# Late x transposes by DMA, K chunks of 128 rows, and score fills shared by two head groups, in a gated attention and MLP kernel on one core

## The chip, the cores and the metric

The kernel runs on one core of one Trainium2 chip. The metric is the device time of one launch in microseconds (us), lower is better. Engines are called PE (TensorE), PEld (its weight loads), DVE (VectorE), ACT (ScalarE), POOL (GpSimd) and SP (SyncE, whose queue issues most DMAs).

## The reference, cut to what matters

```python
# x: 2048 tokens of 448 numbers, bfloat16; 16 heads of 28; four segments of 512 tokens
g = sigmoid((x * gate_w).sum(-1))
a = memory_attention(x, wq, wk, wv, wo, beta)
b = token_mlp(x, w1, b1, w2, b2)
return g * a + (1 - g) * b

# memory_attention, per segment s and head:
logits = q @ k.T / sqrt(28) + causal mask; p = softmax(logits); a_dot = p @ v
a_mem  = phi(q) @ M / (phi(q) @ z)            # phi(t) = t + 1 if t > 0 else exp(t)
o      = sigmoid(beta) * a_mem + (1 - sigmoid(beta)) * a_dot
M += phi(k).T @ v;  z += phi(k).sum()          # carried to the next segment
# then o @ wo

# token_mlp: over the token axis, S = 2048 -> F = 1792 -> S
h = layernorm(x);  u = gelu(h.T @ w1 + b1);  y = u @ w2 + b2
```

The input of the MLP is x itself, so the MLP's first matmul needs only the layernorm of x and the first block of W1. It is the large independent pool of PE work (224 matmuls of the first, 224 to 238 of the second layer) that the kernel places between the pieces of attention.

## The kernel before

The program is written as a list of operations with priorities. A list scheduler in the kernel's own source, with assumed durations, fixes the order on every engine when the program is built. Each engine is given its order as a fixed list: if one operation is late, what stands behind it on that engine is late too (the ACT lines at 28 us, further down, show a wait of 0.74 us passed on in this way).

x is loaded in natural layout (128 tokens on the partitions). Its transpose, needed by the Q, K and V projections, is made on PE against an identity, in four groups of 512 tokens, and copied out of PSUM, the memory that PE writes to, by DVE or ACT. The 448 rows of the contraction are cut in four chunks of CK = 112.

```python
def transposes(tc):                                   # tc = 0..3
    for half in range(2):
        ...
        for ti, c in parts:                           # 8 matmuls
            last = e.matmul(tb[0:CK, at : at + 128], xh[:, 4 * tc + ti, c * CK : c * CK + CK], ident[:, :],
                            is_transpose=True, ...)
        ...                                           # copy of 112 x 1024 by DVE or ACT
```

The layernorm works in place on the same tiles xh, hence after the transposes. One step on POOL computes the coefficients for all sixteen tiles.

```python
def ln_stats(t):  DVE: bn_stats(st6[:, t, :], xh[:, t, :]); bn_aggr(mv[:, t, :], st6[:, t, :])
def ln_coef():    POOL: vpe = var + 1e-5; rstd = vpe ** -0.5; nmr = -mean * rstd      # 128 x 16, all tiles
def ln_apply(t):  DVE: xh[:, t, :] = xh[:, t, :] * rstd[:, t] + nmr[:, t]
```

Attention runs in 16 units, u = (segment, group of 4 heads). Four heads share PE as row tiles of 32 rows, each writing its own PSUM bank of 512 columns. A unit has 1280 causal columns per head and needs three fills of the four banks: 512, 384 + 128, and only 256 in the last. ACT takes the exponential of each fill into an SBUF buffer P (two halves, by parity of u), POOL masks the diagonal blocks, and PE, as column tiles of 32, multiplies P with v.

```python
def scores(n):
    u, f = divmod(n, 3)                               # three fills per unit
    ...
    PE : for j, c0, w_ in segs(f): for hl in range(4): matmul(bank(hl)[:, c0 : c0 + w_], kT[...], qT[...])
    ACT: activation(pv, ps[:, 0:4, 0:w], Exp, scale=SCALE)          # 128 x 2048 or 128 x 1024
    POOL: affine_select(...)                                        # the diagonal blocks
def pv_unit(u): ...                                   # P @ v, the memory term, normalisation, transpose
```

## Time and profile before

| | before |
|---|---|
| time, median of 3 runs (range) | 189.0 us (188.65 to 189.43) |
| profiled execution, span | 186.4 us |
| PE, DVE, ACT busy | 97%, 83%, 72% |
| exponentials, number and busy time | 48, 76.9 us |
| PE transposes of x | 64 |
| first projection, first MLP matmul start | 7.80 us, 34.29 us |

The first part of the page gives busy time, share of the span and number of instructions of each engine.

```profile
PE 180.6 (97%) x1373; PEld 87.3 (47%) x1384; DVE 154.0 (83%) x319; ACT 133.5 (72%) x171; POOL 69.6 (37%) x93
```

The chain that ended last, before: the share of the span that each engine, and each line, has on it.

```profile
PE 82%; DVE 6%; ACT 6%; DMA 3%; issue 1%; SPq 0%
PE t L889 24%; PE t L917 24%; PE t L589 9%; PE t L783 7%; PE t L869 6%; PE t L820 6%; PE t L646 3%; ACT t L792 3%; DMA t<-in_A_wk_dram 3%; DVE t L732 2%; PE t L670 1%; ACT t L631 1%; PE t L558 1%; DVE t L581 1%; DVE t L624 1%
```

So PE sets the time. But "97% busy" is not "97% streaming". The Trainium skill, "Trainium Kernel Development and Optimization", Performance Expectations, calls matmul busy time a bad metric because matmuls are pipelined, and this trace agrees: a matmul of 448 columns is shown with 353 ns, while the next starts 189 ns later. The useful account is made from the starts. I took every matmul of the trace as its columns at 2.4 per ns (56 ns for a 128-column transpose or a 128-column matmul of the full array, as their starts stand) and called the rest up to the next start a gap. The record of before lacks 11 of its 12 matmuls of the memory term (their weight loads are there, see the groups below); they are put back at 512 columns.

The groups of instructions by line and shape, before. The columns are number, busy us, mean ns, idle time of the engine before them, with what ended it. L792 is the exponential, L558 the PE transpose, L581 and L583 the copies of the late transposes, L806 the memory term.

```profile
L792 ACT ACTIVATE t<-t 128x2048 bf16<-128x2048 f32 x32 | 60.3, 1886 | 9.5 <-PE t L783 9.2
...
L792 ACT ACTIVATE t<-t 128x1024 bf16<-128x1024 f32 x16 | 16.5, 1032 | 3.0 <-PE t L783 3.0
...
L558 PE MATMUL t<-t 128*112 128x128 bf16 x64 | 4.5, 220 | 0.1
...
L583 ACT ACTIVATE t<-t 112x1024 bf16<-112x1024 bf16 x3 | 3.1, 1024 | 0.5 <-PE t L558 0.5
L581 DVE COPY t<-t 112x1024 bf16<-112x1024 bf16 x3 | 2.1, 692 | 0.1
L806 PEld LDWEIGHTS t<-t 128*128 128x128 bf16 x12 | 1.2, 97 | 1.9 <-DVE t L688 0.4 <-issue 0.3 <-POOL t L796 0.2
...
L806 PE MATMUL t<-t 128*128 128x512 bf16 x1 | 0.4, 379 | 0.0
```

The timeline of PE around one score fill, before (start, duration, engine, line, shape, number). The fill streams 384 + 128 columns on four row tiles at once.

```profile
42.64 0.73 PE L889 MATMUL t<-t 128*128 128x448 bf16 x3
43.30 0.40 PE L783 MATMUL t<-t 28*128 28x384 bf16 x8
43.63 0.74 PE L889 MATMUL t<-t 128*128 128x448 bf16 x3
```

The last MLP matmul of the first row starts at 43.02 us and streams to 43.20; the fill starts at 43.30, has streamed 512 columns by 43.53, and the MLP goes on at 43.63. About 0.10 us is lost on the way into the tiled mode and again on the way out. The Trainium skill, "TensorEngine Tiling (Array Packing)", Key Properties, says that a change of the tiling mode drains TensorE; the trace agrees and gives the size.

The start of the chain in order of time, before: wk lands at 6.13 us, DVE copies it into its padded form (L536), then come two copies of the first transposes and the first projection (L589).

```profile
1.31 4.82 DMA t<-in_A_wk_dram
...
6.16 0.63 DVE t L536
6.79 0.34 DVE t L571
...
7.15 0.61 ACT t L574
...
7.80 4.31 PE t L589 x33
```

### The profile page before, as it was taken

To read this page: it belongs to the slowest core of one execution; us is meant where nothing else is said; L and a number is where in the kernel's file an instruction comes from. 1 tells how busy PE (TensorE), PEld (TensorE's weight loads), DVE (VectorE), ACT (ScalarE), POOL (GpSimd) and SP (SyncE) were. 2 spreads that over 40 slices of the span, in tenths; PEclk is the share of its full clock that TensorE was granted. 3 is DMA by queue.
4 is the path that set the end of the run, shared out by engine and by line. 5 is a ranking of instruction groups with operands and counts; after the bars stand their busy time and mean duration, and the time that the engine had idled before them with its cause. 6 is when DMAs were issued, how large, how long until landed. Compare 5 with 4: busy or idle time off the path is not lost.

```text
span 186.4 us, 3493 instructions
## 1 busy us (share of the span) xinstructions
PE 180.6 (97%) x1373; PEld 87.3 (47%) x1384; DVE 154.0 (83%) x319; ACT 133.5 (72%) x171; POOL 69.6 (37%) x93
## 2 busy tenths in 40 slices
PE   7999999999999999999999999999999999999994
PEld 2658434344454444434454443454454444454554
DVE  1979898998689989798998999998999987765232
ACT  2288779968999999999988979840399857620230
POOL 8200029343242534543725635171135365160200
PEclk9999999999999999999999999999999999999999
DMA  3999991001971746001341506238810072744011
GB/s 92 321 328 265 294 150 28 5 0 40 250 220 31 204 116 159 4 4 28 96 133 37 160 4 183 45 102 225 240 35 0 4 213 70 212 146 127 0 53 49
DMA packets 42596, 21.77 MB, mean 117 GB/s; under 512 B 8148, under 2 KB 42580, under 8 KB 42580
## 3 DMA queue, kind: packets, MB, share of 16 engines
q1 hardware_dynamic: 42116, 21.54, 43.7%
q8 instruction: 11, 0.18, 0.4%
q10 hardware_dynamic: 464, 0.00, 0.1%
q14 instruction: 5, 0.04, 0.1%
HBM read 18.13 MB, written 1.84 MB: 107 GB/s over the span
## 4 chain that ended last, share of the span: by engine, by line
PE 82%; DVE 6%; ACT 6%; DMA 3%; issue 1%; SPq 0%
PE t L889 24%; PE t L917 24%; PE t L589 9%; PE t L783 7%; PE t L869 6%; PE t L820 6%; PE t L646 3%; ACT t L792 3%; DMA t<-in_A_wk_dram 3%; DVE t L732 2%; PE t L670 1%; ACT t L631 1%; PE t L558 1%; DVE t L581 1%; DVE t L624 1%
## 5 line engine op out<-in xcount | busy, mean ns | idle before, releaser
L792 ACT ACTIVATE t<-t 128x2048 bf16<-128x2048 f32 (+1 forms) x48 | 76.9, 1601 | 12.5 <-PE t L783 12.2
L796 POOL TENSOR_SCALAR_AFFINE_SELECT t<-t 128x512 bf16<-128x512 bf16 x64 | 47.0, 737 | 64.2 <-ACT t L792 59.9
L889 PE MATMUL t<-t 128*128 128x448 bf16 x224 | 47.3, 353 | 0.4 <-issue 0.3
L917 PE MATMUL t<-t 128*128 128x448 bf16 (+1 forms) x238 | 46.0, 342 | 0.3
L917 PEld LDWEIGHTS t<-t 128*128 128x128 bf16 x238 | 22.2, 98 | 19.4 <-issue 1.7
L589 PE MATMUL t<-t 112*128 112x512 bf16 (+1 forms) x144 | 30.0, 356 | 0.4 <-ACT t L574 0.4
L889 PEld LDWEIGHTS t<-t 128*128 128x128 bf16 x224 | 20.2, 98 | 20.4 <-issue 2.6
L849 POOL TENSOR_TENSOR t<-t 128x448 bf16<-128x448 f32 x12 | 14.3, 1196 | 18.2 <-DVE t L847 18.2
L589 PEld LDWEIGHTS t<-t 112*128 112x128 bf16 x144 | 13.4, 98 | 13.1 <-issue 0.9
L922 DVE SCALAR_TENSOR_TENSOR t<-t 128x448 bf16<-128x448 f32 (+1 forms) x17 | 11.1, 653 | 10.0 <-PE t L917 7.5
L783 PE MATMUL t<-t 28*128 28x512 bf16 (+3 forms) x256 | 17.3, 302 | 0.8 <-ACT t L792 0.3
L875 ACT ACTIVATE t<-t 128x448 bf16<-128x448 f32 x9 | 6.6, 730 | 12.4 <-PE t L869 12.2
L646 PE MATMUL t<-t 112*128 112x449 bf16 x64 | 14.1, 354 | 0.1
L869 PE MATMUL t<-t 128*128 128x448 bf16 x64 | 13.6, 353 | 0.0
L835 DVE STREAM_TRANSPOSE t<-t 128x512 f32<-128x512 f32 x16 | 11.3, 703 | 2.6 <-PE t L820 2.6
L626 ACT ACTIVATE t<-t 128x512 bf16<-128x512 f32 x8 | 4.8, 595 | 11.4 <-PE t L589 11.4
L783 PEld LDWEIGHTS t<-t 28*128 28x128 bf16 x256 | 5.1, 91 | 16.3 <-ACT t L792 10.8
L855 DVE STREAM_TRANSPOSE t<-t 128x512 bf16<-128x512 bf16 x16 | 11.2, 698 | 1.6 <-POOL t L849 1.6
L732 DVE BATCH_NORM_STATS2 t<-t 128x6 f32<-128x448 bf16 x16 | 9.4, 611 | 3.5 <-DMA t<-in_A_x_dram 3.3
L820 PE MATMUL t<-t 128*32 128x512 bf16 (+3 forms) x256 | 11.6, 302 | 0.0
L906 DVE SCALAR_TENSOR_TENSOR t<-t 128x448 bf16<-128x448 f32 x14 | 9.2, 658 | 2.9 <-ACT t L904 2.8
L901 DVE SCALAR_TENSOR_TENSOR t<-t 128x448 f32<-128x448 f32 x14 | 9.7, 697 | 1.7 <-ACT t L896 1.7
(83 smaller groups left out, 216.1 us busy)
## 6 DMA issues: line engine op xcount, KB each, us to landing
t<-in_B_w_dram SPq DMA_DIRECT2D x7, 1024.0 KB, 6.0
t<-in_B_w_dram SPq DMA_DIRECT2D x8, 896.0 KB, 5.2
out_dram<-t SPq DMA_DIRECT2D x15, 112.0 KB, 3.0
t<-in_A_x_dram SPq DMA_DIRECT2D x3, 448.0 KB, 7.7
t<-in_A_x_dram SPq DMA_DIRECT2D x2, 224.0 KB, 4.4
t<-in_A_wk_dram SPq DMA_DIRECT2D x1, 392.0 KB, 4.8
t<-in_A_wq_dram SPq DMA_DIRECT2D x1, 392.0 KB, 5.8
t<-in_A_wv_dram SPq DMA_DIRECT2D x1, 392.0 KB, 6.6
```

Source lines behind the costliest of these rows:

```text
L589: last = e.matmul(bank(b)[:, 0:n], w_pad[0:CK, c, hg * 128 : hg * 128 + 128], xT[0:CK, c, tc * 512 + t0 : tc * 512 + t0 + n], start=(c == ...
L646: last = e.matmul(bank(b)[:, 0 : D + 1], xT[0:CK, c, t * 128 : t * 128 + 128], wvx[0:CK, c, :], start=(c == 0), stop=(c == NCT - 1), skip_ ...
L732: op("DVE", lambda e: e.bn_stats(st6[:, t, :], xh[:, t, :]), reads=[R_x[t]], writes=[R_st6[t]], name=f"bns{t}", cost=512, prio=P_PROJ - 10)
L783: last = e.matmul(bank(hl)[:, c0 : c0 + w_], kT[r, hg, s * 512 + j * 128 : s * 512 + j * 128 + 128], qT[r, hg, s * 512 + 128 * j : s * 512 ...
L792: op("ACT", lambda e: e.activation(pv, ps[:, 0:4, 0:w], ACT.Exp, scale=SCALE), reads=R_bank[0:4], writes=[R_P[u % 2][f]], name=f"exp{n}", ...
L796: op("POOL", lambda e, d=d: e.affine_select(d, d, pattern=[[0, 4], [1, 128]], compare_op=ALU.is_ge, fill=0.0, base=0, channel_multiplier=- ...
L820: last = e.matmul(bank(cb)[32 * hl : 32 * hl + 32, 128 * j : 512], vaug[:, 4 * s + j, 32 * h : 32 * h + 32], pv[:, hl, c0 : c0 + w_], star ...
L835: dv(lambda e: e.transpose(t2[:, 0, :], bank(cb)[:, 0:512]), [bres(cb)], [R_tt[tb][0]], "ta", 630, use=(cb,))
L849: op("POOL", lambda e: e.tensor_tensor(o3, n3[0], n3[1], op=ALU.add), reads=R_tt[tb], writes=[R_ob[tb]], name=f"o{u}", cost=1280, port=Tru ...
L869: last = e.matmul(bank(b)[:, 0:D], oT[:, hg, T * 128 : T * 128 + 128], wo_sb[:, hg, :], start=(hg == 0), stop=(hg == NHG - 1), skip_group_ ...
L889: op("PE", lambda e, st=st: e.matmul(bank(b)[:, 0:D], w1c[:, st, f2 * 128 : f2 * 128 + 128], xh[:, st, :], start=(st == 0), stop=(st == NT ...
L917: op("PE", lambda e, ft=ft: e.matmul(bank(b)[:, 0 : c1 - c0], w2c[:, ft, t2_ * 128 : t2_ * 128 + 128], uT[:, ft, c0:c1], start=(ft == 0), ...
```

## The change

The intent: take PE time away. Half of the PE transposes (tokens 1024 to 2047) become transposing DMAs from DRAM, written here in chunks of 128 columns: the 448 are covered by chunks at 0, 128, 256 and 320, the last overlaps by 64 rows, and zeros in the weights cancel the overlap. Each weight is therefore loaded in two DMAs. And two units share five fills of 512 columns instead of six, of which two were half empty; the exponentials go to five P buffers from a pool.

```diff
-CK = 112
+CK = 128
+C0 = (0, 128, 256, 320)
...
+    def load_w(dst, src, r, name, take=None):
+        op("SP", lambda e: e.dma_start(dst()[:, 0:3, 0:D], src[0:384].rearrange("(c p) d -> p c d", p=128)), ...)
+        op("ACT", lambda e: e.dma_start(dst()[64:128, 3, 0:D], src[384:448]), ...)
+
+    def transpose_x(tc):
+        for k, (c, n) in enumerate(((0, 3), (3, 1))):
+            op("SP", lambda e, c=c, n=n: e.dma_start_transpose(
+                xT[:, c : c + n, tc * 512 : tc * 512 + 512], x2[tc * 512 : tc * 512 + 512, C0[c] : C0[c] + 128 * n]),
+               writes=[R_xT[tc][k]], name=f"dtx{tc}_{k}", dma=True, cost=1200 * n, nbytes=180000 * n)
...
     load_x("SP", 0, 2)
-    op("SP", ... wk ...)
+    load_w(wk_nat, WK, R_wk, "wk", P_wk)
     load_x("SP", 2, 2)
-    op("ACT", ... gate weights ..., name="ldgw")
-    op("SP", ... wq ...)
-    op("SP", ... wv ...)
+    load_w(wq_nat, WQ, R_wq, "wq", P_wq)
+    load_w(lambda: wvx, WV, R_wv, "wv")
+    op("ACT", ... gate weights, rows 0 to 383 ..., name="ldgw")
+    op("ACT", ... gate weights, rows 384 to 447 ..., name="ldgwb")
+    for w, r, name in (...): op("DVE", lambda e, w=w: e.memset(w()[0:64, 3, :], 0.0), ...)
...
-    def segs(f):
-        return [(0, 0, 512)] if f == 0 else ([(1, 0, 384), (3, 384, 128)] if f == 1 else [(2, 0, 256)])
+    FILLS = (((0, 0, 0, 512),), ((0, 1, 0, 384), (0, 3, 384, 128)), ((0, 2, 0, 256), (1, 2, 256, 256)),
+             ((1, 0, 0, 512),), ((1, 1, 0, 384), (1, 3, 384, 128)))
+    P_fill = [[Bank("p") for _ in FILLS] for _ in range(8)]
...
-    for tc in (1, 2, 3):
-        transposes(tc)
+    transposes_1()
...
+    transpose_x(2)
+    transpose_x(3)
...
-        for f in range(3):
-            scores(3 * u + f)
+        for f in ((0, 1, 2), (3, 4))[u % 2]:
+            scores(u // 2, f)
```

## The prediction

> **What bounds the kernel now.** TensorE. The page gives PE 97% of the 186.4 us span, and the chain of waits is 82% PE; DVE is busy 83%, ACT 72%. Counting each matmul by its start and its columns at 2.4 per ns (448-column matmuls start every 189 ns), only about 20 us of the span are not streaming. About 8 us of that is the start, some 10 us are entries to and exits from the tiled attention matmuls, and only eight holes are longer than 0.25 us. In the timeline at 43 us, a fill of four score banks streams 512 columns in 0.21 us but takes 0.43 us of PE from the last MLP matmul before it to the first after it: about 0.11 us is lost going in and again coming out. The Trainium skill, "TensorEngine Tiling (Array Packing)", Key Properties, says that changing the tiling mode drains TensorE; these gaps agree (0.10 to 0.12 us each, more when ACT is late).
>
> **What the change removes.**
> 1. Fills: 48 become 40, with the same columns. 8 x (0.11 + 0.11) = 1.8 us of PE.
> 2. PE transposes of x: 64 become 32. They start 56 ns apart in the trace: 1.8 us of PE, between 14 and 18 us, on the chain.
> 3. Four of six PSUM copies of those transposes (1.02 us each on ACT, 0.69 us on DVE). The layernorm of x on DVE, which releases the first MLP matmul at 34.3 us, can end about 1 us sooner.
> 4. Exponentials: 32 x 1.88 + 16 x 1.03 = 76.7 us become 40 x 1.88 = 75.2 us of ACT. Mostly off the chain (it runs over ACT from 78 to 87 us).
>
> **What it adds.** Four transposing DMAs from DRAM on SP's queue. The present twelve (128x512) take 1.2 us to issue and 2.4 to 2.6 us to land; I estimate 3.6 us of issue for the three-chunk ones, about 10 us of SP in all, and 1 MB more traffic in the first 35 us. The first three W1 blocks land at 19.1, 24.0 and 27.3 us and are needed from 34 us on; the transposed x is needed only after 70 us. So this should hide. Each weight now comes in two DMAs, the second from ACT; wk's landing (6.13 us) is on the chain and may slip by 0 to 0.4 us. Three DVE memsets (0.27 us) fall in idle time. Chunks of 128 rows stream the same columns; the masks stay 64; five P buffers hold as much as before.
>
> **Sum.** -1.8 - 1.8 + 0.2, and some small holes less: about -3.6 us, nearly all on the chain as PE is saturated. Predicted 185.4 us, 8 in 10 between 183.6 and 187.4. That is 1.9% less, so the 2% line is almost a coin toss: faster 0.44, same 0.51, slower 0.05.
>
> **What would show it.** Right: span near 182.8; PE busy about 3.5 us less at the same 97%; 40 exponentials of 1.88 us; PE transposes x32; first MLP matmul 1 to 2 us before 34.3; gaps per fill unchanged.
>
> **What would make it wrong.** The transposing DMAs issue or land far slower, hold back SP's W1 loads or the phi(K) transposes, and ACT stalls on the two-buffer phi(K); a late second half of wk; the list scheduler's new order leaving PE holes (plus or minus 1 us); or fills in pairs letting more score and PV work stand together, saving more switches than 16.

## More of the kernel before

The granted TensorE clock is 0.999 or 1.000 in all profiles.

The timeline of PE where the MLP begins, before: L646 is a V projection, L589 a Q or K projection, L783 a fill, L889 the first MLP layer; the two lines left out are one more fill and the first P @ v.

```profile
30.57 0.29 PE L783 MATMUL t<-t 28*128 28x256 bf16 x4 [0.32 <-ACT t L792]
30.79 1.71 PE L646 MATMUL t<-t 112*128 112x449 bf16 x8
32.34 1.02 PE L589 MATMUL t<-t 112*128 112x512 bf16 x4
...
34.29 1.45 PE L889 MATMUL t<-t 128*128 128x448 bf16 x6
```

The windows view gives busy time of each engine in a stretch; here 12 to 28 us and 60 to 90 us, before.

```profile
12.00:28.00 16.00, 16.00 (x123) 8.79 (x122) 15.10 (x63) 12.70 (x22) 0.99 (x2) 1.00 1.09 239
...
60.00:90.00 30.00, 29.62 (x238) 12.95 (x241) 27.24 (x49) 29.09 (x41) 13.23 (x16) 1.00 0.32 84
```

The columns after the length are PE, PEld, DVE, ACT, POOL, clock, DMA share and GB/s. DVE is busy 15.10 of 16 us in the first stretch.

## The result, and the profile after

| | before | changed |
|---|---|---|
| time, median of 6 runs (range) | 189.28 us (188.65 to 189.69) | 186.47 us (186.34 to 187.14) |
| ratio of fast runs, 95% interval | | 0.9861 (0.9837 to 0.9885) |
| span of the profiled execution | 186.4 us | 184.6 us |
| first projection, first MLP matmul | 7.80, 34.29 us | 7.34, 31.64 us |

Ratios are the mean time of one kernel's fast runs over that of the other's of the same rounds, so they are not quite the ratio of the medians quoted. The change takes 1.4% off, about 2.6 us. 186.47 us lies in the predicted range of 183.6 to 187.4, and "within 2%" was the likeliest of the three forecasts; but 1.0 us of the predicted 3.6 us is missing (0.8 us by the medians). The two profiles differ by only 1.8 us, because the profiled execution of before took 188.43 us, less than any of its six timed ones. What follows compares the two profiles and keeps this in mind.

The parts of the page that answer to those of before: busy times, and the chain.

```profile
PE 178.6 (97%) x1352; PEld 84.7 (46%) x1352; DVE 153.2 (83%) x321; ACT 132.0 (71%) x160; POOL 72.9 (39%) x93
```

```profile
PE 70%; DVE 17%; ACT 5%; POOL 3%; DMA 2%; issue 1%; SPq 0%
PE t L959 23%; PE t L931 17%; PE t L626 9%; PE t L824 5%; PE t L911 5%; PE t L861 5%; PE t L683 4%; DMA t<-in_A_wk_dram 2%; ACT t L833 2%; DVE t L769 2%; POOL t L779 2%; DVE t L948 1%; DVE t L943 1%; DVE t L941 1%; PE t L847 1%; DVE t L921 1%
```

PE is as busy as before, 97%. But its share of the chain fell from 82% to 70%, and that of DVE rose from 6% to 17%.

The groups after: L833 is the exponential, L578 and L607 the PE transposes that are left, L620 their ACT copies, L847 the memory term, now fully recorded.

```profile
L833 ACT ACTIVATE t<-t 128x2048 bf16<-128x2048 f32 x40 | 75.3, 1883 | 9.7 <-PE t L824 9.5
...
L847 PE MATMUL t<-t 128*128 128x512 bf16 x12 | 4.6, 383 | 0.1
...
L620 ACT ACTIVATE t<-t 128x1024 bf16<-128x1024 bf16 x2 | 2.1, 1034 | 0.0
...
L578 PE MATMUL t<-t 128*128 128x128 bf16 x16 | 1.2, 219 | 0.0
L607 PE MATMUL t<-t 128*128 128x128 bf16 x16 | 1.2, 218 | 0.0
```

The account of the span from the starts of the matmuls, in us. A change of the tiling mode is counted at 0.10 us; "other gaps" is what remains of the gaps.

| | before | changed | difference |
|---|---|---|---|
| start, to the first projection | 7.80 | 7.34 | -0.46 |
| columns streaming | 160.88 | 159.05 | -1.83 |
| changes of the tiling mode | 115 x 0.10 = 11.5 | 96 x 0.10 = 9.6 | -1.9 |
| other gaps | 3.55 | 5.93 | +2.38 |
| ... of these in the first 36 us | 1.22 | 2.76 | +1.54 |
| tail behind the last matmul | 2.70 | 2.69 | 0 |
| span | 186.43 | 184.61 | -1.82 |

What was meant to be removed is removed, to the size that was meant: 32 transposes, and even 19 changes of mode rather than 16. Out of 4.2 us gained so (0.46 + 1.83 + 1.9), 2.4 us came back as gaps in which PE waits: 1.54 us in the first 36 us, 0.84 us after. The largest stand where the MLP begins. The timeline of PE after (L683 is a V projection, L824 a fill, L931 the first MLP layer):

```profile
27.95 2.46 PE L683 MATMUL t<-t 128*128 128x449 bf16 x12
31.32 0.39 PE L824 MATMUL t<-t 28*128 28x512 bf16 x4 [0.90 <-ACT t L697]
31.64 0.55 PE L931 MATMUL t<-t 128*128 128x448 bf16 x2
32.40 0.55 PE L931 MATMUL t<-t 128*128 128x448 bf16 x2 [0.20 <-DVE t L785]
```

The twelve projections have streamed by about 30.25 us (12 x 187 ns after 27.95 with a short gap), and PE does nothing for 1.07 us up to the fill, then waits again for the layernorm products of DVE (L785). The fill names ACT (L697) as what released it. ACT was late because of DVE, as its own timeline shows: L668 is the exponential for phi(q), L661 the copy of q by DVE that it waits for, L833 the exponential of the fill before, which ends at 31.27 us, just before the new fill starts in the same banks.

```profile
28.27 1.23 ACT L668 ACTIVATE t<-t 128x512 bf16<-128x512 bf16 x2 [0.74 <-DVE t L661]
...
29.41 1.86 ACT L833 ACTIVATE t<-t 128x2048 bf16<-128x2048 f32 x1
```

A second new hole, 0.57 us at 16.0 us, ends with another copy of DVE (L641). The windows after:

```profile
12.00:28.00 16.00, 15.60 (x104) 7.13 (x103) 14.85 (x64) 13.29 (x23) 3.24 (x2) 1.00 1.12 252
...
60.00:90.00 30.00, 29.63 (x242) 12.46 (x234) 29.96 (x50) 27.85 (x33) 13.97 (x19) 1.00 0.22 52
```

DVE still works 14.85 of 16 us between 12 and 28 us, where PE has less to do now, and it has next to no idle time between 60 and 90 us (29.96 of 30 us). One group of float32 products on DVE, which occurs 14 times, runs 0.1 us longer than before on average (658 ns became 783 ns). The Trainium skill, "SBUF — State Buffer", SBUF: two separate sides, describes a port pair that DVE and POOL take from each other as an exclusive lock. Five of the fourteen are slow, 1.05 to 1.07 us each; they do overlap a mask of POOL by 0.57 to 0.59 us each, but so do some that are not slow, and no run here tests that cause.

The start of the chain after:

```profile
1.29 3.74 DMA t<-in_A_wk_dram
...
5.05 1.28 DVE t L561
6.33 0.34 DVE t L591
...
6.69 0.60 ACT t L594
...
7.34 4.74 PE t L626 x35
```

The transposing DMAs of the changed kernel, from the part on DMA issues: number and median time from issue to landing.

```profile
t<-t SPq DMA_TRANSPOSE x12, 2.5
...
t<-in_A_x_dram SPq DMA_TRANSPOSE x4, 5.2
```

The first three W1 blocks land at 23.1, 26.6 and 29.9 us instead of 19.1, 24.0 and 27.3 us. They are still there before the first MLP matmul at 31.64 us.

### The profile page after: what moved, and what is told of

The parts are those of the page before. It is cut to its first block, busy times and chain, and to the rows that moved or that the text cites. A ratio compares the mean times of both kernels' runs of the same rounds, so it can differ in the third digit from the quotient of the medians.

```text
span 184.6 us, 3441 instructions
## 1 busy us (share of the span) xinstructions
PE 178.6 (97%) x1352; PEld 84.7 (46%) x1352; DVE 153.2 (83%) x321; ACT 132.0 (71%) x160; POOL 72.9 (39%) x93
## 4 chain that ended last, share of the span: by engine, by line
PE 70%; DVE 17%; ACT 5%; POOL 3%; DMA 2%; issue 1%; SPq 0%
PE t L959 23%; PE t L931 17%; PE t L626 9%; PE t L824 5%; PE t L911 5%; PE t L861 5%; PE t L683 4%; DMA t<-in_A_wk_dram 2%; ACT t L833 2%; DVE t L769 2%; POOL t L779 2%; DVE t L948 1%; DVE t L943 1%; DVE t L941 1%; PE t L847 1%; DVE t L921 1%
## 5 line engine op out<-in xcount | busy, mean ns | idle before, releaser
L833 ACT ACTIVATE t<-t 128x2048 bf16<-128x2048 f32 x40 | 75.3, 1883 | 9.7 <-PE t L824 9.5
L836 POOL TENSOR_SCALAR_AFFINE_SELECT t<-t 128x512 bf16<-128x512 bf16 x64 | 49.3, 771 | 53.7 <-ACT t L833 46.5
L931 PE MATMUL t<-t 128*128 128x448 bf16 x224 | 47.3, 353 | 0.3 <-DVE t L785 0.2
L959 PE MATMUL t<-t 128*128 128x448 bf16 (+1 forms) x238 | 45.1, 342 | 0.0
L959 PEld LDWEIGHTS t<-t 128*128 128x128 bf16 x238 | 22.7, 98 | 19.6 <-issue 1.7
L626 PE MATMUL t<-t 128*128 128x512 bf16 (+1 forms) x144 | 30.5, 356 | 0.9 <-DVE t L641 0.4
L931 PEld LDWEIGHTS t<-t 128*128 128x128 bf16 x224 | 20.2, 98 | 21.3 <-issue 3.9
L891 POOL TENSOR_TENSOR t<-t 128x448 bf16<-128x448 f32 x12 | 15.0, 1249 | 22.0 <-DVE t L889 22.0
L626 PEld LDWEIGHTS t<-t 128*128 128x128 bf16 x144 | 13.1, 98 | 14.5 <-DVE t L641 1.5
L824 PE MATMUL t<-t 28*128 28x512 bf16 (+3 forms) x256 | 15.8, 301 | 1.0 <-ACT t L697 0.9
L683 PE MATMUL t<-t 128*128 128x449 bf16 x64 | 13.7, 353 | 0.0
L948 DVE SCALAR_TENSOR_TENSOR t<-t 128x448 bf16<-128x448 f32 x14 | 10.8, 783 | 1.3 <-ACT t L946 1.3
L861 PE MATMUL t<-t 128*32 128x512 bf16 (+3 forms) x256 | 11.3, 302 | 0.0
L824 PEld LDWEIGHTS t<-t 28*128 28x128 bf16 x256 | 4.4, 92 | 14.3 <-ACT t L833 8.0
L663 ACT ACTIVATE t<-t 128x512 bf16<-128x512 f32 x10 | 5.9, 594 | 5.3 <-PE t L626 5.3
```

The source lines that it names most:

```text
L626: last = e.matmul(bank(b)[:, 0:n], w_pad[0:CK, c, hg * 128 : hg * 128 + 128], xT[0:CK, c, tc * 512 + t0 : tc * 512 + t0 + n], start=(c == ...
L683: last = e.matmul(bank(b)[:, 0 : D + 1], xT[0:CK, c, t * 128 : t * 128 + 128], wvx[0:CK, c, 0 : D + 1], start=(c == 0), stop=(c == NCT - 1 ...
L824: last = e.matmul(bank(hl)[:, c0 : c0 + w], kT[r, hg, s * 512 + j * 128 : s * 512 + j * 128 + 128], qT[r, hg, s * 512 + 128 * j : s * 512 ...
L833: op("ACT", lambda e: e.activation(pslot(g), ps[:, 0:4, :], ACT.Exp, scale=SCALE), reads=R_bank[0:4], writes=[g.res], take=g, name=f"exp{p ...
L836: op("POOL", lambda e, c0=c0: e.affine_select(pslot(g)[:, :, c0 : c0 + 128], pslot(g)[:, :, c0 : c0 + 128], pattern=[[0, 4], [1, 128]], co ...
L861: last = e.matmul(bank(cb)[32 * hl : 32 * hl + 32, 128 * j : 512], vaug[:, 4 * s + j, 32 * h : 32 * h + 32], pslot(P_fill[u // 2][f])[:, h ...
```

## The experiments

Theory A: PE time freed early meets engines that the change left alone, mainly DVE, and turns into waits. A1 blames the layernorm's power on POOL; A2 says that DVE is simply full in the first 32 us. Rival B: the transposing DMAs hold back W1 or the transposes of phi(K). Rival C: sharing the fills is worth little in itself. All times are medians, all kernels correct unless said.

| run | time, us | ratio to before (95%) | other gaps, us |
|---|---|---|---|
| changed kernel | 186.47 | 0.9861 (0.9837 to 0.9885) | 5.93 |
| e1_fills | 188.01 | 0.9964 (0.9949 to 0.9979) | 4.95 |
| e2_xpose | 187.57 | 0.9939 (0.9923 to 0.9955) | 5.15 |
| e3_dtx_late | 186.71 | 0.9891 (0.9873 to 0.9908) | 5.94 |
| e6_gw_first | 187.76 | 0.9948 (0.9932 to 0.9964) | 5.92 |
| e8_before_gw_late | 188.13 | 0.9977 (0.9965 to 0.9990) | 3.55 |
| e4_pow_short (wrong result) | 186.77 | 0.9892 (0.9877 to 0.9907) | 5.95 |
| e5_stats_half (wrong result) | 184.90 | 0.9806 (0.9793 to 0.9820) | 4.32 |
| e13_before_stats_half (wrong result) | 187.99 | 0.9970 (0.9956 to 0.9984) | 3.01 |
| e9_dve_light (wrong result) | 186.11 | 0.9875 (0.9861 to 0.9888) | 5.43 |
| e10_gw_behind | 186.70 | 0.9882 (0.9866 to 0.9899) | 6.08 |
| e11_ln_halves | 184.82 | 0.9794 (0.9776 to 0.9812) | 4.29 |
| e12_small_late | 184.37 | 0.9763 (0.9743 to 0.9783) | 3.38 |

The records of e4, e5 and e9 lack twelve matmuls whose weight loads are there, eight of the memory term and four of projections; they are put back at 512 columns, as for before. The changed kernel itself was not timed again in the later groups of runs; e3, which has its order on all engines but SP and turned out the same, and e10 stand in for it there at 0.988 to 0.989.

### e1_fills: the fills alone

```diff
 # the kernel before, with only FILLS, the shared scores() and the pool of five P buffers; CK = 112, loads as before
```

> Only the shared score fills and the pool of five P buffers; the loads, the chunks of 112 rows and all PE transposes are those of before. Theory A (the change fell short because the PE time freed early meets DVE and the layernorm, which do not get faster; fills are worth what I said): 40 exponentials, some 16 to 19 fewer changes of the tiling mode at 0.1 us, 1.5 to 1.9 us less than before, about 187.5 us. Rival C (sharing fills itself brings new waits in the attention stretch and is worth little): less than 0.7 us gained, above 188.5 us, with the holes after 60 us of the changed kernel present here too.

Measured: 97 changes of mode instead of 115, so 1.8 us were removed as planned, and 40 exponentials. But the time fell by only 0.7 us by the ratio (0.36%), 0.9 us by the medians (188.89 to 188.01 in the runs beside it): the other gaps rose from 3.55 to 4.95 us. Some are at the start of the MLP (0.48 us at 33.8, 0.37 us at 35.3 us), some late (0.45 us at 93.5, 0.60 us at 139.5 us). Neither number was met: A had expected 1.5 to 1.9 us, C a time above 188.5 us. C was nearer: its gain of less than 0.7 us is met by the ratio, though not by the medians. But the late holes are not those of the changed kernel (there 0.41 us at 77.3 and 0.26 us at 114.9 us), and this run's order was planned anew: whether the sharing or the new order brings the waits is not separated.

### e2_xpose: the transposes, the chunks and the loads alone

```diff
 # the changed kernel, with segs(), three fills per unit and the two P halves of before
```

> Only the late transposes by DMA, chunks of 128 and split weight loads; 48 fills and the two P halves of before. Theory A: 1.8 us of PE transposes and 0.46 us of start are removed, but the first 36 us show new holes on PE of about 1 us or more behind DVE and ACT, so that 0.8 to 1.5 us remain: 187.8 to 188.4 us. Rival B (the transposing DMAs get in the way of other transfers): also short, but the waits of the first 36 us name DMAs. If A and B are both wrong the full 2.3 us are there: 187.0 us.

Measured: 1.15 us less than before by the ratio (0.61%). The gain is inside what A expected, 0.8 to 1.5 us; the time itself lies just below A's range, as the kernel before took 188.89 us in the runs beside it. The first projection starts at 7.35 us; in the first 36 us the gaps beyond the changes of mode are 2.79 us, as large as the 2.76 us of the whole change. No wait of PE after the first transposes names a DMA. The two parts together give 1.0% by their ratios, the whole change 1.1 to 1.4%: they add up about, with nothing hidden between them.

### e3_dtx_late: the transposing DMAs out of the way

```diff
     sch.plan()
+    # the four transposing DMAs of x move behind the W1 loads and the first two phi(K) transposes on SP
+    sch.ops = rest[:k] + late + rest[k:]
```

> The changed kernel with the same order on every engine but SP, where the four transposing DMAs of x are issued behind the W1 loads and the first two phi(K) transposes. Theory A: no effect, within 0.3 us of the changed kernel (186.2 to 186.8 us), though W1 lands some 4 us sooner. Rival B (transposing DMAs hold back W1 or phi(K)): at least 0.8 us faster than the changed kernel and the hole of 1.1 us at 31 us shrinks.

Measured: 186.71 us, within 0.3 us of the changed kernel, and in the profile the same span, 184.6 us, and the same holes (1.07 us at 31.3, 0.37 us at 32.4 us) to 0.01 us. W1 lands sooner (20.3, 23.9 and 27.1 us) and nobody notices. Rival B falls. The Trainium skill, "DMA: Bandwidth & Descriptors", Rules for kernel authors, says that a transposing DMA next to ordinary ones needs no precaution; that is a rule about right results, and the results here agree. That it costs no time here either is shown by e3.

### e6_gw_first and e8_before_gw_late: the place of a 0.9 KB load

```diff
 # e6: the changed kernel, ACT's queue in the order
+ldgw, ldgwb, wk (second part), wq (second part), wv (second part)
-wk (second part), wq (second part), wv (second part), ldgw, ldgwb
 # e8: the kernel before, ldgw moved from the first place on ACT's queue to behind wv on SP's
```

> The changed kernel with the two element-wise loads of the gate weights issued first on ACT, as before, instead of behind the weights; nothing else is moved. If the sooner start of the changed kernel (first projection at 7.34 instead of 7.80 us) comes from these small packets having left the way of wk, then wk lands near 6.1 us again instead of 5.0, wq sooner than 9.3 us, the first projection starts at about 7.8 us, and the time is 0.2 to 0.5 us longer. If the start came from the split of the weights, nothing changes (within 0.2 us).

> The kernel before, in its own order, with the element-wise load of the gate weights issued behind the three weight matrices on the loading queue instead of first on ACT. Since the gate load's place moved the changed kernel by 1.1 us, expect here: wk lands at about 5 us instead of 6.13, the first projection starts 0.4 to 0.8 us sooner than 7.80, and the time falls by 0.4 to 0.8 us (188.2 us): that part of the changed kernel's gain would belong to neither of its two ideas. If the split of the weight loads is what made the start sooner, nothing changes here.

Measured: e6 has the same order otherwise and the same other gaps, but its first projection starts at 8.64 instead of 7.34 us and its time is 1.0 to 1.3 us longer (187.76 against 186.71 and 186.47), more than expected. The start of its chain:

```profile
1.89 5.03 DMA t<-in_A_wk_dram
...
7.00 0.63 DVE t L561
```

The second part of wk now stands behind the element-wise loads on ACT's queue and lands at 6.91 instead of 3.90 us; this is the "late second half of wk" that the prediction had as a risk. e8 shows the other side: with the gate load out of the way in the kernel before, wk lands at 5.47 instead of 6.13 us, the first projection starts at 7.35 us, and 0.4 us are gained (0.23%). The start of the changed kernel, 7.34 us, is not sooner than that. So the whole gain at the start, 0.46 us, is explained by the gate load's place and belongs to neither idea of the change; splitting the weights cost nothing as long as the gate load came after. The Trainium skill, "DMA: Bandwidth & Descriptors", Issuing engines are not separate DMA queues, says that DMAs of different engines' queues share the same DMA engines and interleave; the trace agrees, as a load of 0.9 KB on ACT's queue delayed a load of 392 KB on SP's by 0.66 us in the two profiled executions (wk lands at 6.13 to 6.20 us in all three profiles with the gate load first and wk in one piece: before, e1 and e13); the timed runs, with 0.4 us, are the safer number.

### e4_pow_short, e5_stats_half and e13_before_stats_half: what holds the first 32 us

All three keep the order of their kernel on every engine. Their outputs are wrong, which doesn't matter for the times.

```diff
 # e4, on the changed kernel
-po(lambda e: e.tensor_tensor(rstd[:], vpe[:], mhalf[:], op=ALU.pow), ..., "rstd")
+po(lambda e: e.tensor_tensor(rstd[:], vpe[:], mhalf[:], op=ALU.mult), ..., "rstd")
 # e5, on the changed kernel, and e13, on the kernel before
-e.bn_stats(st6[:, t, :], xh[:, t, :])
+e.bn_stats(st6[:, t, :], xh[:, t, 0:112])
```

> WRONG RESULT on purpose. The changed kernel in its own order on every engine, with the power of the layernorm's variance (2.92 us on POOL) replaced by a product (0.2 us). Theory A1 (the hole of 1.1 us at 31 us and the two behind it come from the layernorm's chain through POOL): the first layernorm product on DVE comes sooner than 29.99 us and the holes of the first 36 us shrink by 1 us or more, the time by as much (about 185.5 us). Theory A2 (DVE and ACT are full in that stretch and simply late, the power is not what they wait for): the holes stay within 0.4 us, and so does the time (186.1 to 186.6 us).

> WRONG RESULT on purpose. The changed kernel in its own order on every engine; the sixteen BATCH_NORM_STATS of the layernorm read 112 of the 448 columns (about 0.25 us instead of 0.61), which takes some 5 us from DVE between 4 and 24 us and nothing else. Theory A2 (DVE is full in the first 32 us): the holes at 16.5 and 31 us shrink by 1 us or more and the time falls by about as much, to about 185.4 us. Theory A1 (power on POOL): vpe starts sooner here too, so the holes shrink as well; the two are told apart by the run with the short power. If neither holds, the time stays within 0.3 us.

> WRONG RESULT on purpose. The kernel before, in its own order on every engine, with the sixteen BATCH_NORM_STATS of the layernorm on 112 of the 448 columns, as was done to the changed kernel, where it gained about 1.6 us. Theory A2 in its full form (DVE in the first 32 us became the limit only because the change shortened PE's part there): here it gains less than 0.8 us (above 188.1 us, ratio above 0.996), since PE has only 0.5 us of holes in that stretch. Rival: the stretch was bound by DVE all along; then it gains 1.2 us or more here too (ratio below 0.994), and the change merely did not help it.

Measured: taking 2.7 us from the power gains nothing (186.77 us; ratio 0.9892, as e3). Its profiled execution was its slowest (187.84 us; the second x tiles landed late, at 8.24 us, and the first projection began at 8.75 us), but the other gaps are those of the changed kernel, 5.95 us in all and 2.78 us in the first 36 us (5.93 and 2.76), with a hole of 1.5 us before the first MLP matmul. A1 falls. Taking work from DVE gains 1.0 to 1.8 us: 184.90 us against 186.47 and the stand-ins' 186.7, or 0.9806 against 0.986 to 0.989. The low end is the comparison by ratio with the changed kernel, 0.55% of 189 us. In its profile the hole at 31 us is gone, and the MLP runs without a break; the hole of 0.57 us at 16.0 us, which the expectation named too, is still there. The other gaps of the first 36 us fall from 2.76 to 1.18 us, those after stay (3.16 and 3.14 us). The timelines of PE and, before the fill, of ACT in e5:

```profile
29.82 0.54 PE L683 MATMUL t<-t 128*128 128x449 bf16 x2
30.38 0.39 PE L824 MATMUL t<-t 28*128 28x512 bf16 x4
30.71 2.25 PE L931 MATMUL t<-t 128*128 128x448 bf16 x11
```

```profile
26.91 1.66 ACT L668 ACTIVATE t<-t 128x512 bf16<-128x512 bf16 x3
...
28.46 1.86 ACT L833 ACTIVATE t<-t 128x2048 bf16<-128x2048 f32 x1
```

ACT no longer waits for the copy of q, and the exponential in front of the fill starts at 28.46 instead of 29.41 us.

The same relief in the kernel before gains 0.5 us (0.3%), about its one hole at 30.6 us; there the gaps of the first 36 us fall from 1.22 to 0.67 us. This pair is the clearest result: the same 5 us of DVE work are worth 0.5 us with the PE work of before and two to three times as much with the lighter PE work of the change. In the changed kernel DVE is the limit of that stretch; in the kernel before it was so for only 0.5 us. The change brought less PE work and a newly planned order together; the pair shows what both did, and doesn't separate the two.

### e9_dve_light: the waits after 60 us

```diff
 # on the changed kernel, order kept, wrong result: tanh argument and the two normalisations on a quarter of their columns
-e.scalar_tensor_tensor(gg[:, q, :], gg[:, q, :], 1.0, vh[:, q, :], ...)
+e.scalar_tensor_tensor(gg[:, q, 0:112], gg[:, q, 0:112], 1.0, vh[:, q, 0:112], ...)
```

> WRONG RESULT on purpose. The changed kernel in its own order on every engine; three float32 products on DVE in the attention and MLP stretch (the argument of the tanh, the two normalisations) work on a quarter of their columns, some 15 us less DVE work between 36 and 165 us. The first 36 us stay as they are. Theory D (the waits of PE that the changed kernel has after 60 us and before has not, about 1.1 us in 60 to 120 us, are behind a late DVE): they shrink by 0.7 us or more and the time falls by 0.7 to 1.5 us. Rival (they are behind ACT, in the exponentials, or in the order itself): within 0.3 us.

Measured: 186.11 us, 0.1 to 0.6 us less than the changed kernel and its stand-ins; the gaps beyond changes of mode fell from 1.15 to 0.49 us between 60 and 90 us, and stayed at 0.9 us between 90 and 120 us. After 36 us they fell from 3.16 to 2.51 us in all. So a part of the later waits is behind DVE and another part is not. Neither expectation is met cleanly. What the rest waits for stays open; two runs below show that a new order removes most of it.

### e10_gw_behind, e11_ln_halves and e12_small_late: relieving DVE with a correct result

```diff
 # e10: both gate loads on SP's queue behind wv, order kept
 # e11: coefficients of the layernorm for tiles 0 to 7 and 8 to 15 apart
-ln_coef()
+for i in range(2): ln_coef(i)
 # e12: nineteen tiny DVE instructions (rows, maskg) that are needed after 50 us
+late = name[:2] in ("rw", "rv", "me", "mg", "mo")
-op("DVE", fn, reads=reads, writes=writes, name=name, cost=100, prio=pr, rel=15000.0)
+op("DVE", fn, reads=reads, writes=writes, name=name, cost=100, prio=pr, rel=34000.0 if late else 15000.0)
```

> The changed kernel in its own order, with both gate-weight loads issued from the loading queue behind the last weight matrix, instead of from ACT in front of it. In the changed kernel wq lands at 9.3 us and DVE idles 0.96 us for it, in the stretch where DVE is full. Theory A2 (DVE in the first 32 us is what the freed PE time meets): wq lands 1 us or more sooner, the idle goes, the hole at 31 us shrinks by 0.5 us or more, the time falls by 0.4 to 0.9 us against the changed kernel (ratio to before about 0.983). If the gate loads matter only through wk: nothing (within 0.2 us).

> The changed kernel with the layernorm's coefficients computed for tiles 0 to 7 as soon as their statistics are there, and for 8 to 15 later; the order is planned anew. With the late transposes off the x tiles, nothing but the one common coefficient step holds the first MLP matmul. Theory A2: more MLP work is ready when PE runs out of projections, so the holes behind 31 us go (1 to 1.4 us) and the time falls by 0.7 to 1.3 us against the changed kernel (ratio to before 0.979 to 0.983). Rival: the new order pays it back elsewhere, within 0.3 us of the changed kernel.

> The changed kernel with nineteen tiny DVE instructions, which set up the mask of the memory matrix and are needed only after 50 us, kept back until about 34 us; the order is planned anew. They take about 2.5 us from a full DVE between 16 and 24 us. Theory A2: the DVE work of the layernorm ends sooner, the hole at 31 us shrinks by 0.7 us or more, the time falls by 0.6 to 1.2 us against the changed kernel (ratio to before 0.980 to 0.984). Rival: within 0.3 us.

Measured, e10: wq lands at 7.39 instead of 9.30 us, as expected, and nothing is gained (186.70 us; the hole at 31.5 us is still 1.06 us). wk landed later in the profiled execution (5.84 us; among the profiles with the gate load behind the weights it varies from 4.9 to 6.0), and the start with it by 0.17 us. DVE's idle time for wq was not what mattered.

e11: 184.82 us, a ratio of 0.979 as A2 expected, but not by its mechanism: a hole of 1.3 us is still there at 32.1 us. The gaps of the first 36 us are 2.50 us (2.76 before), and the gain comes after 60 us, where the newly planned order has gaps of 0.37 us where the changed kernel has 1.15 (60 to 90 us) and 0.35 where it has 0.90 (90 to 120 us).

e12: 184.37 us, 2.4% less than before and 1.1% less than the changed kernel by the medians: the best version found, correct, and faster than both. The timeline of its PE:

```profile
29.75 0.92 PE L683 MATMUL t<-t 128*128 128x449 bf16 x4
30.51 0.54 PE L932 MATMUL t<-t 128*128 128x448 bf16 x2
31.30 0.39 PE L825 MATMUL t<-t 28*128 28x512 bf16 x4 [0.26 <-ACT t L697]
31.63 1.69 PE L932 MATMUL t<-t 128*128 128x448 bf16 x8
```

The MLP starts before the fill, and the hole in front of the fill is 0.42 us instead of 1.07. DVE works 14.12 us between 12 and 28 us, 0.7 us less. In the account the gaps of the first 36 us fall from 2.76 to 1.42 us, those after 36 us from 3.17 to 1.96 us. The hole shrank by 0.65 us where 0.7 us or more was expected; the time fell by more than expected. About half of the gain lies in the first 36 us, where the theory puts it, and half lies after, where, apart from the nineteen small instructions moved there, only the order changed. How much of the first half is the order too, this run doesn't separate.

## Why the prediction was right or wrong

**The total.** 186.47 us against a prediction of 185.4 us and a range of 183.6 to 187.4: inside, on the slow side. "Within 2%" was right. The gain was 2.6 us instead of 3.6 us. Some luck is in it: the gate load's place, which the prediction had not seen, gave about 0.4 us of these 2.6 us (e8).

**"8 x (0.11 + 0.11) = 1.8 us of PE": the removal was right, its worth was not.** Changes of mode fell from 115 to 96, 1.9 us at 0.10 us each; 0.11 was a little high. Alone on the chip this part gave 0.7 us (e1), because 1.4 us came back as other gaps.

**"1.8 us of PE, between 14 and 18 us, on the chain": the size was right (1.83 us of streaming), the place only partly.** The transposing part with its loads gave 1.15 us alone (e2), of which 0.4 us is the place of the gate load by e8.

**"The layernorm ... can end about 1 us sooner": it did better, and it was not enough.** Its first product came at 29.99 instead of 32.34 us and the first MLP matmul at 31.64 instead of 34.29 us, 2.65 us sooner where 1 to 2 were expected. But PE was sooner still, and stood still for 1.07 us and, just after, 0.37 and 0.23 us.

**The step that failed is in the sum: "nearly all on the chain as PE is saturated".** It takes PE's saturation as given while it removes PE work. With about 4 us less for PE (4.2 us in the account), DVE, at 15.1 of 16 us between 12 and 28 us, became the limit of the first 32 us: e5 and e13 show this, with 1.0 to 1.8 us against 0.5 us for the same relief. Instead of "some small holes less", there were 2.4 us more of gaps. Of these, 1.54 us lie in the first 36 us, and e5 takes that much away there (1.58 us). The 0.84 us after 36 us are not DVE's alone: e9 takes 0.65 us away, and e11, which leaves the work there as it is and changes the order, 1.4 us. The prediction had the new order among its risks ("PE holes (plus or minus 1 us)"), but not in its sum.

**"+0.2" for the start: wrong sign.** wk came at 5.03 instead of 6.13 us and the start was 0.46 us sooner. I had seen the second DMA of each weight and not that the gate load moved behind them (e6, e8).

**Right:** the exponentials (40 of 1.88 us, 75.3 us), the transposes (32), PE still at 97%, the gaps per fill unchanged at 0.10 us, and that the transposing DMAs hide (e3). Their issue took 11.3 us of SP in all (3.36, 4.35, 2.31 and 1.26 us), near the estimate of 10, but by luck: in e3, issued behind the loads, three chunks take 1.5 us and one takes 1.26, 5.6 us in all, so about half of the 11.3 us was waiting and the estimate of the issue itself was too high. **Wrong:** "span near 182.8" (184.6). **Not far off:** "PE busy about 3.5 us less": the pages show 2.0 us, but that of before lacks 11 matmuls; with them put back at the 383 ns of L847 its busy time is about 181.7 us, an estimate, and the difference 3.1 us.

**Open:** what the later gaps that e9 did not remove wait for, how much of e12's gain is only its order, and how much of the waits of the first 32 us comes from the lighter PE work and how much from the order planned with it.

## What to carry to other kernels

When one engine is saturated and another is at 94% in the same stretch, price the removal of work from the first only up to the second: read the busy time of all engines in that stretch, not the share over the span, and ask who will be waited for next. With an order that is fixed when the program is built, test a suspected limit by making its instructions shorter and keeping the order, on both kernels; the difference between the two is the part that the change, its new order included, caused. And check where tiny element-wise loads stand in the DMA queues at the start: here the place of a 0.9 KB load moved the time by 0.4 to 1.3 us.

## What the Trainium skill lacked or had wrong

- "TensorEngine Tiling (Array Packing)", Key Properties, says that a mode change drains TensorE but gives no cost: 0.10 us for each change here, 9.6 to 11.5 us per launch.
- "DMA: Bandwidth & Descriptors" does not give, in microseconds and for these shapes, the issue time of a transposing DMA on SP: 1.2 us for 128 x 512 from SBUF, 1.26 us for one chunk of 512 x 128 from DRAM, and 1.53 to 1.55 us for three chunks (e3, behind the loads), up to 4.35 us with loads ahead; 5.2 us median from issue to landing for the four from DRAM.
- The same page's rule on non-contiguous runs speaks of the slow load itself, not of its neighbours: 448 elements of 2 bytes, issued first, delayed wk (392 KB, on another queue) from 5.47 to 6.13 us in the profiled executions, and the launch by 0.4 us (e8).
- "Perfetto Trace Analysis" does not warn that a trace may lack matmuls whose weight loads it has: 11 of 12 of the memory term in the record of before, and twelve matmuls in those of e4, e5 and e9. Gaps and busy counts must be corrected for it.
